# Attention scores, row steps and exponentials in another block order, with a look-ahead of one key tile and half of the scores split

## The chip, the core and the metric

The kernel runs on one core of one Trainium2 chip. The metric is the device time of one execution, in microseconds (us). The kernel before was timed in 3 runs: median 1334.1 us, lowest 1333.32, highest 1335.31.

## What is computed

One input `x` of 2048 rows and 512 columns goes through two branches, and a gate per row mixes them:

```python
# attention: 32 query heads of 16 columns share one key and one value head
q = (x @ wq).reshape(B, S, H, Dh); k = x @ wk; v = x @ wv
p = softmax(einsum("bhqd,bkd->bhqk", q, k) * Dh ** -0.5)
a = einsum("bhqk,bkd->bhqd", p, v).reshape(B, S, H * Dh) @ wo
# feed-forward, F = 1792
b = (silu(x @ w_gate) * (x @ w_up)) @ w_down
g = sigmoid((x * gate_w).sum(-1))
return g * a + (1 - g) * b
```

All in float32. The softmax is taken without subtracting a maximum; a flag computed beside it decides whether a slow path has to run, and it does not run here.

## The kernel before

**Tiles.** The kernel works head by head (32 heads) on key tiles of 128 keys, 16 to a head, numbered `u` from 0 to 511. For each `u` the scores of 128 keys against 2048 queries are needed. They are made in two score tiles (`j` = 0 and 1) of 1024 queries, each by two matmuls of 64 rows that run side by side (L727, output `pss`, one PSUM tile of two banks; there are two such tiles in rotation). ScalarE takes the exponential of a score tile into `pt` (L735). When a `u` is complete, the *mix* multiplies `pt` with the values and a column of ones and adds up into `po` (L747): four matmuls that run side by side in four column groups, each in two passes.

**Kinds.** A score tile is of kind A or H. Kind A: one exponential of 1024 columns from PSUM. Kind H (split): VectorE copies the second 512 columns out of PSUM into `pt` (L731), ScalarE takes the exponential of the first 512 from PSUM, and later of the other 512 in place in `pt`. The PSUM tile is free for the score tile after next once its exponential from PSUM and, for kind H, the copy are done.

**Feed-forward.** The feed-forward work and the query projections are cut into *jobs* of 12 or 15 matmuls (gate, up, down; L196, output `pf`, three PSUM tiles in rotation). During attention each matmul is cut into two halves of 64 rows: one *step* F runs a low half of one job beside a high half of another. The class `Halves` holds this pipeline: a low half starts when one of three tickets in `free` is due (7 clocks after a high half closed), and its high half starts `LAG` = 8 clocks after the low half's end; a 1x1 VectorE memset (`sign`, L470) orders the two. When a high half closes, VectorE takes `pf` out of PSUM (L299, L327, L390, L392); a list `HOLD` puts this behind the copy of a split score tile that comes within two steps.

**Order of the work.** It is written out by hand. `STEPS` is a string of 8 S (one score tile) and 16 F (one step) for a block of four key tiles; `KINDS` gives the kinds of its 8 score tiles, numbered 0 to 7; `EXPS` the order of the exponentials on ScalarE ("1d" from PSUM, "1s" in place, "|" the end of the block's steps). After the steps come ScalarE's tanh of the feed-forward, as much postponed VectorE work as fits a budget (`LATER`: normalization of a finished head; `DEFER`: silu, casts), then the mix of four key tiles. A block that mixes `u` to `u+3` scores `u+2` to `u+5`: the look-ahead is two key tiles. The first 32 key tiles run in a simpler loop of two key tiles; the block at the turn (`TURN`) scores five key tiles to build up the look-ahead; 118 blocks follow that are alike, and a last one that scores two.

**Stores in SBUF.** Six `pt` buffers (3 in `bp`, 3 in `bp2`), and three row chunks of the feed-forward sum `acc`; the fourth use of `acc` takes the place of chunk 0, which is stored to DRAM and read back at the end.

**The end.** Jobs that are left run with 128 rows. The last head is normalized, goes to DRAM and comes back transposed into chunks (L499), which ScalarE or GpSimd splits into a high and a low part (L501, L503, L504), and the output projection runs chunk by chunk (L118, L519).

Of the kernel before, what the change touches and what calls it, by code (L numbers as in the profile page):

```python
# [8 lines left out]
F32 = mybir.dt.float32  # L9
# [39 lines left out]
WRB = 2  # L49
BLOCK = 4  # L50
BEGIN = 16
STOP = 2
EARLY = 6
OUTS = (1, 2, 3, 0)
STEPS = "SSFFFFFSFSFFFSFFSFFFFFSS"
KINDS = "AHHAHAAA"
EXPS = ("0d", "1d", "2d", "3d", "4d", "5d", "1s", "4s", "2s", "|", "6d", "7d")
TURN = "SSFFFFSFS" + "FFS" * 5 + "FS"
BUDGET = 3.8
AHEAD = 6  # L60
# [3 lines left out]
def tile_gated_mix(ctx, tc, x, wq, wk, wv, wo, w_gate, w_up, w_down, gate_w, out):  # L64
# [213 lines left out]
    def open_acc():  # L278
        qpool.release()
        for name in ("accp", "bp2"):  # L280
            PAIR.append(tc.alloc_tile_pool(name=name, bufs=3, side="right"))

    def gate_up(n, c):
# [9 lines left out]

        def gate(ps):
            g = wp.tile([P, CH], F32, name="hs", bufs=2)
            if n == SPLIT:
# [102 lines left out]


    def jobs():
        late = []
        for m, c in enumerate(ORDER):
            for fs in GROUPS:
                ns = [m * NF + f for f in fs]
                new = [job for n in ns for job in gate_up(n, c)]
                if late and ns[-1] < NCH * NF - 1:
                    late[-1].after.append(lambda ns=ns: LOADS.extend([lambda n=n: load_w("d", n) for n in ns]))
                if fs[-1] == NF - 1:
                    if m < 2:  # L410
                        new[-1].after.append(lambda m=m: load_x_again(ORDER[m + 2]))
                for j, job in enumerate(new):
# [26 lines left out]
    class Halves:  # L439
# [6 lines left out]
        def step(self, more):  # L446
            for i in range(1, min(AHEAD, len(JOBS))):
                if not JOBS[0].ready() and JOBS[i].ready():
                    JOBS.insert(0, JOBS.pop(i))
            if (not self.low and JOBS and JOBS[0].ready() and (JOBS[0].only is None) == more and  # L450
                    self.free and min(self.free) <= self.clock):
                self.free.remove(min(self.free))
                self.low = [JOBS.pop(0), 0]
            if self.early and self.steps >= 4:
# [51 lines left out]
    def finish(c, pool):  # L506
        for i in range(TC):
# [3 lines left out]
            for j in range(parts):  # L511
# [7 lines left out]
                nc.vector.scalar_tensor_tensor(ot[:, w], ps[:, :D // parts], g_sb[:, t:t + 1], ACC[c][:, i, w],  # L519
                                               op0=ALU.mult, op1=ALU.add)  # L520
# [188 lines left out]
    with tc.tile_pool(name="bpool", bufs=2) as bp:  # L709
# [59 lines left out]
        NU = H * NT  # L769
        NB = NU // BLOCK  # L770
        COPY = []

        def feed(k, more=True):
            for _ in range(k):
                if JOBS and more or halves.busy():
                    halves.step(more)

        def block(k, first, last, steps, kinds, order):
            more = k < NB - STOP
# [4 lines left out]
            def emit():  # L784
                while order and order[0] != "|" and int(order[0][0]) < len(made):
                    i, how = int(order[0][0]), order.pop(0)[1]
                    pt, ps, other = made[i]
# [21 lines left out]
            assert not order and len(made) == len(tiles)  # L809
            left = BUDGET  # L810
            rest = NT // BLOCK - k % (NT // BLOCK)
            for _ in range(-(-len(LATER) // rest) if DEFER else 2):
                if LATER:
# [13 lines left out]
            FRESH.clear()  # L827
            for u in range(BLOCK * k, BLOCK * (k + 1)):
                mix(u)
            halves.clock += 2 * LONG  # L830

# [6 lines left out]
        with tc.manual_schedule():  # L838
# [24 lines left out]
            assert PAIR  # L863
            for k in range(2 * BEGIN // BLOCK, NB):
                u = BLOCK * k
                if k == 2 * BEGIN // BLOCK:
                    n = u + 6 - (u + 1)
                    block(k, u + 1, u + 6, TURN, "A" * 2 * n, [f"{i}d" for i in range(2 * n)])
                elif k == NB - 1:
                    block(k, u + 2, u + 4, STEPS, "AAAA", ("0d", "1d", "2d", "3d", "|"))  # L870
                else:
                    block(k, u + 2, u + 6, STEPS, KINDS, EXPS)
                h = u // NT
                if k % (NT // BLOCK) == 0 and 0 < h < H - 1:
                    load_head(h + 1)
# [9 lines left out]
    with tc.tile_pool(name="tpool", bufs=2) as tp, tc.tile_pool(name="rpool", bufs=1, side="right") as rp, \  # L885
# [112 lines left out]
```

## Time and profile before

| | us |
|---|---|
| median of 3 runs | 1334.1 |
| span of the profiled execution | 1332.6 |
| outside the span (median less span) | 1.5 |
| VectorE copies of split score tiles | 354, 692 ns each |
| exponentials from PSUM, 1024 columns / 512 columns | 670 / 354 |
| exponentials in place, 512 columns | 354 |
| longest wait of ScalarE, in total | 140.5, for scores |

The start (transposes, key and value projection, first query projections) takes some 49 us, the loop over the first 32 key tiles ends at 129, the blocks at 1260.6, and the end takes the remaining 72 us. In the chain of waits "PE po L747 x32" is the mix of one block, so the distance from one such row to the next is the time of a block. In a timeline a row holds the start, the duration, the engine, the line, the operation and in brackets how long the engine was idle before it and what ended that.

### The profile page before, as it was taken

How to read it: one execution, taken by the hardware profiler on the slowest of the kernel's cores; microseconds unless marked ns; L12 is line 12 of the kernel's file. 1: busy time of each engine (PE TensorE's matmuls, PEld its weight loads, DVE VectorE, ACT ScalarE, POOL GpSimd, SP SyncE). 2: the span in 40 equal slices, each digit the busy share in tenths (PEclk: the TensorE clock that was granted, in tenths of full speed). 3: DMA queues.
4: the chain of work that ended last, by engine and by line, in shares of the span. 5: the costliest groups of instructions: out<-in, count | busy, mean ns of one | idle time of the engine just before them, and what ended most of it. 6: DMA issues, size and time to landing. Idle time of an engine off the chain costs nothing.

```text
span 1332.6 us, 26698 instructions
## 1 busy us (share of the span) xinstructions
PE 1322.7 (99%) x10767; PEld 761.9 (57%) x10767; DVE 712.2 (53%) x1220; ACT 1069.0 (80%) x1475; POOL 225.4 (17%) x229
## 2 busy tenths in 40 slices
PE   9999999999999999999999999999999999999998
PEld 7655555555555555555555555555555555555587
DVE  4655565565546565555555555455455455546542
ACT  4578888888888888888888888888888888888601
POOL 5350221142032151142010000000000000001043
PEclk9999999999999999999999999999999999999999
DMA  8677021131125372264044342143132342143164
GB/s 286 206 227 241 27 61 36 45 92 53 45 93 176 113 241 68 92 211 138 33 134 161 103 159 84 53 145 102 37 114 64 104 161 82 52 147 108 39 207 151
DMA packets 101937, 156.29 MB, mean 117 GB/s; under 512 B 11824, under 2 KB 43312, under 8 KB 100144
## 3 DMA queue, kind: packets, MB, share of 16 engines
q1 hardware_dynamic: 100080, 154.31, 35.9%
q8 instruction: 88, 1.44, 0.5%
q10 hardware_dynamic: 1728, 0.20, 0.1%
q14 instruction: 41, 0.34, 0.1%
HBM read 98.37 MB, written 55.57 MB: 116 GB/s over the span
## 4 chain that ended last, share of the span: by engine, by line
PE 97%; ACT 1%; DVE 1%; issue 0%; DVEq 0%; ACTq 0%
PE pf L196 38%; PE po L747 34%; PE pss L727 20%; PE pf L118 4%; ACT pt L735 1%; PE pss L613 0%; PE po L600 0%; DVE xl L618 0%; PE pss L653 0%; DVE acc L390 0%; DVE ht L327 0%; DVE hs L299 0%; DVE wkv_l L109 0%; DVE pt L731 0%; ACT xh L617 0%
## 5 line engine op out<-in xcount | busy, mean ns | idle before, releaser
L735 ACT ACTIVATE pt<-pss 128x1024 f32<-128x1024 f32 (+1 forms) x1024 | 842.0, 876 | 173.7 <-PE pss L727 140.5
L731 DVE COPY pt<-pss 128x512 f32<-128x512 f32 x354 | 244.8, 692 | 419.8 <-PE pss L727 386.8
L747 PE MATMUL po<-pt,vaug 128*32 128x512 f32 x4096 | 467.6, 595 | 0.0
L727 PE MATMUL pss<-qs,ks 64*128 64x512 f32 x2048 | 395.1, 415 | 0.8 <-ACT pt L735 0.5
L727 PEld LDWEIGHTS pss<-qs,ks 64*128 64x128 f32 x2048 | 188.3, 184 | 220.1 <-ACT pt L735 183.8
L747 PEld LDWEIGHTS po<-pt,vaug 128*32 128x32 f32 x4096 | 119.2, 109 | 260.1 <-issue 254.9
L735 ACT ACTIVATE pt<-pt 128x512 f32<-128x512 f32 x354 | 195.6, 620 | 0.0
L196 PE MATMUL pf<-xh,wgl 64*128 64x512 f32 (+1 forms) x444 | 163.4, 392 | 0.0
L196 PE MATMUL pf<-xh,wgh 64*128 64x512 f32 (+1 forms) x444 | 161.8, 392 | 0.3
L196 PE MATMUL pf<-xl,wgh 64*128 64x512 f32 (+1 forms) x444 | 161.4, 390 | 0.0
L196 PE MATMUL pf<-xh,wuh 64*128 64x512 f32 (+1 forms) x440 | 158.4, 392 | 0.5 <-DVE sign L470 0.3
L196 PE MATMUL pf<-xl,wuh 64*128 64x512 f32 (+1 forms) x440 | 157.7, 390 | 0.0
L196 PE MATMUL pf<-xh,wul 64*128 64x512 f32 (+1 forms) x440 | 157.0, 391 | 0.0
L196 PE MATMUL pf<-wdh,hl 64*128 64x512 f32 (+1 forms) x411 | 137.0, 390 | 0.0
L196 PE MATMUL pf<-wdh,hh 64*128 64x512 f32 (+1 forms) x411 | 136.7, 391 | 0.0
L196 PE MATMUL pf<-wdl,hh 64*128 64x512 f32 (+1 forms) x411 | 136.6, 390 | 0.0
L756 DVE RECIPROCAL rsb<-rsb 128x128 f32<-128x128 f32 x128 | 116.9, 934 | 10.9 <-issue 8.8
L501 POOL CAST xh<-wraw 128x512 fp32r<-128x512 f32 x4 | 2.9, 726 | 505.2 <-DMA wraw<-o_d 505.2
L196 PEld LDWEIGHTS pf<-xh,wgh 64*128 64x128 f32 (+1 forms) x444 | 79.0, 185 | 8.8 <-issue 1.0
L196 PEld LDWEIGHTS pf<-xl,wgh 64*128 64x128 f32 (+1 forms) x444 | 79.1, 185 | 6.3
L196 PEld LDWEIGHTS pf<-xh,wuh 64*128 64x128 f32 (+1 forms) x440 | 77.1, 185 | 9.7 <-issue 2.1
L196 PEld LDWEIGHTS pf<-xh,wgl 64*128 64x128 f32 (+1 forms) x444 | 79.1, 185 | 5.7
(168 smaller groups left out, 1388.3 us busy)
## 6 DMA issues: line engine op xcount, KB each, us to landing
qs<-q_d SPq DMA_DIRECT2D x31, 512.0 KB, 5.1
q_d<-hh SPq DMA_DIRECT2D x28, 256.0 KB, 3.8
wraw<-in_B_w_gate_dram SPq DMA_DIRECT2D x28, 256.0 KB, 3.4
wraw<-in_B_w_up_dram SPq DMA_DIRECT2D x28, 256.0 KB, 3.1
wraw<-in_B_w_down_dram SPq DMA_DIRECT2D x28, 256.0 KB, 3.7
wgh<-w_d SPq DMA_DIRECT2D x28, 256.0 KB, 2.8
wgl<-w_d SPq DMA_DIRECT2D x28, 256.0 KB, 3.0
wuh<-w_d SPq DMA_DIRECT2D x28, 256.0 KB, 2.7
```

Of the source, the lines that this page charges most:

```text
L118: nc.tensor.matmul(ps, a, b, start=(i == 0), stop=(i == n - 1))
L196: ins = nc.tensor.matmul(self.ps, a, b, start=(i == 0 and opens), stop=(last and closes))
L501: nc.gpsimd.tensor_copy(OT[c][0][:, k, :], raw)
L727: nc.tensor.matmul(ps[:, b * CH:(b + 1) * CH], ks[rows, kt * P:(kt + 1) * P], QS[h][rows, j, :], start=True, stop=True)
L731: other = nc.vector.tensor_copy(pt[:, CH:], ps[:, CH:]) if half else None
L735: ins = nc.scalar.activation(pt[:, w], ps[:, w], AF.Exp, scale=SCALE)
L747: nc.tensor.matmul(po[c * 2 * DH:(c + 1) * 2 * DH, :], vaug[:, kt, :], pt[:, c * CH:(c + 1) * CH], start=(kt == 0), stop=(kt == NT - 1))
L756: nc.vector.reciprocal(rsb[:, w], rsb[:, w])
```

## The change

- The look-ahead goes from two key tiles to one: a block that mixes `u` to `u+3` scores `u+1` to `u+4`. The block at the turn scores four key tiles instead of five and has 12 F instead of 16; the last block scores three instead of two and goes on with full F steps (`STOP` 2 to 1; `feed` no longer stops when `more` is false).
- Split tiles are 1, 2, 5 and 6 instead of 1, 2 and 4. The sixth S stands one F later. The exponentials come in the order 0d 1d 2d 3d 4d 5d 5s 1s 2s, then, after the tanh, 6d 7d 6s. (The "T" in the table runs the tanh list, which is empty by then.)
- `pt` has seven buffers instead of six (`bp2` 4), `acc` two chunks instead of three. Chunk 1 is read back from DRAM into four buffers of the up weights at the end (`acc_again`), and the output chunks come in the order 2, 3, 1, 0 instead of 1, 2, 3, 0.
- The two loads of a row chunk (`load_x_again`) are no longer issued at once but put at the end of the list `LOADS`, behind down weights that wait there.
- A gate's end first runs postponed work of two feed-forward tiles earlier; a low half is picked from the first job that is ready; the VectorE budget goes from 3.8 to 3.87.

```diff
-OUTS = (1, 2, 3, 0)
-STEPS = "SSFFFFFSFSFFFSFFSFFFFFSS"
-KINDS = "AHHAHAAA"
+OUTS = (2, 3, 1, 0)
+STEPS = ("SSFFFFFSFSFFFSFFFSFFFFSS",)
+KINDS = ("AHHAAHHA",)
...
     def load_x_again(c):
         if c in ORDER:
-            for j, part in enumerate(new_x(c)):
-                nc.sync.dma_start(part.bitcast(F32), x_d[c - 2, j])
+            LOADS.extend([lambda j=j, part=part: nc.sync.dma_start(part.bitcast(F32), x_d[c - 2, j])
+                          for j, part in enumerate(new_x(c))])
...
-        for name in ("accp", "bp2"):
-            PAIR.append(tc.alloc_tile_pool(name=name, bufs=3, side="right"))
+        for name, bufs in (("accp", ACCS), ("bp2", PTL)):
+            PAIR.append(tc.alloc_tile_pool(name=name, bufs=bufs, side="right"))
...
         def gate(ps):
+            while any(item[0] <= n - 2 for item in DEFER):
+                run(ACTS, len(ACTS))
+                i = min(i for i, item in enumerate(DEFER) if item[0] <= n - 2)
+                DEFER.pop(i)[2]()
...
+    def acc_again():
+        c = ORDER[NCH - ACCS - 1]
+        ACC[c] = [wp.tile([P, KD, P], F32R, name="wu" + x, bufs=2).bitcast(F32).rearrange("p k f -> p (k f)")
+                  for x in "hhll"]
+        for i in range(TC):
+            nc.sync.dma_start(ACC[c][i], a_d[c, :, i, :])
...
-            for i in range(1, min(AHEAD, len(JOBS))):
-                if not JOBS[0].ready() and JOBS[i].ready():
-                    JOBS.insert(0, JOBS.pop(i))
...
+            if not self.low and self.free and min(self.free) <= self.clock:
+                for i in range(min(AHEAD, len(JOBS)) if more else len(JOBS)):
+                    if JOBS[i].ready() and (JOBS[i].only is None) == more:
+                        self.free.remove(min(self.free))
+                        self.low = [JOBS.pop(i), 0]
+                        break
...
-            late = u > PTB * (BEGIN * 2 // PTB) and (u - 2 * BEGIN) % (2 * PTB) >= PTB
-            PT[u] = (PAIR[1] if late else bp).tile([P, S], F32, name="pt", bufs=PTB)
+            late = u > 2 * BEGIN and (u - 2 * BEGIN) % (PTB + PTL) >= PTB
+            PT[u] = (PAIR[1] if late else bp).tile([P, S], F32, name="pt", bufs=PTL if late else PTB)
...
-                    block(k, u + 2, u + 6, STEPS, KINDS, EXPS)
+                    block(k, u, n, u + 1, end, STEPS[k % len(SIZES)], KINDS[k % len(SIZES)], EXPS[k % len(SIZES)].split())
```

ScalarE's instructions in one of the like blocks before, from tile 6 of the block ahead on (`pt<-pss` is an exponential from PSUM, `pt<-pt` one in place; in brackets the engines whose semaphores an instruction waits for):

```order
L735 ACTIVATE pt<-pss 128x1024 [waits PE_49,Activation_49]
L735 ACTIVATE pt<-pss 128x1024 [waits PE_49] x2
L735 ACTIVATE pt<-pss 128x512 [waits PE_49] x2
L735 ACTIVATE pt<-pss 128x1024 [waits PE_49]
L735 ACTIVATE pt<-pss 128x512 [waits PE_49]
L735 ACTIVATE pt<-pss 128x1024 [waits PE_49]
L735 ACTIVATE pt<-pt 128x512 [waits DVE_49] x2
L735 ACTIVATE pt<-pt 128x512
```

The rows are tile 6, tiles 7 and 0, tiles 1 and 2, 3, 4, 5, and the second halves of 1, 4 and 2. The same engine in one of the like blocks of the changed kernel, from tile 0 on:

```order
L749 ACTIVATE pt<-pss 128x1024 [waits PE_49,Activation_49]
L749 ACTIVATE pt<-pss 128x512 [waits PE_49] x2
L749 ACTIVATE pt<-pss 128x1024 [waits PE_49]
L749 ACTIVATE pt<-pss 128x1024 [waits PE_49,Activation_49]
L749 ACTIVATE pt<-pss 128x512 [waits PE_49]
L749 ACTIVATE pt<-pt 128x512 [waits DVE_49]
L749 ACTIVATE pt<-pt 128x512 x2
L749 ACTIVATE pt<-pss 128x512 [waits PE_49]
L749 ACTIVATE pt<-pss 128x1024 [waits PE_49]
L749 ACTIVATE pt<-pt 128x512 [waits DVE_49]
```

Before, the exponential with two waits is that of tile 6, in all 118 like blocks, and tile 0 has two in 2 of them; now tile 0 has two in 117 of 118, and tile 4 in all. VectorE in one block before, from the copy of tile 1 on (`pt<-pss` are the copies of split tiles; the rest is feed-forward):

```order
L731 COPY pt<-pss 128x512 [waits PE_49]
L731 COPY pt<-pss 128x512 [waits PE_49,Activation_49]
L327 TENSOR_TENSOR ht<-ht,pf 128x512 [waits PE_49]
L731 COPY pt<-pss 128x512 [waits PE_49,Activation_49]
L470 MEMSET sign 1x1 [waits PE_49]
```

And one block of the changed kernel, from the copy of tile 1 on:

```order
L745 COPY pt<-pss 128x512 [waits PE_49,Activation_49]
L745 COPY pt<-pss 128x512 [waits PE_49]
L398 SCALAR_TENSOR_TENSOR acc<-pf,c_sb,acc 128x512 [waits PE_49]
L484 MEMSET sign 1x1 [waits PE_49]
L745 COPY pt<-pss 128x512 [waits PE_49,Activation_49] x2
```

Before, the copy of tile 2 has two waits in 67 of the 118 like blocks, and so has that of tile 4; now the copy of tile 2 has one wait in all of them, and the copies of tiles 5 and 6 have two in 65. On TensorE the feed-forward matmuls behind the last mix are 95 instead of 99: 11 steps that were still in the pipeline and seven jobs, instead of eight jobs.

More of the change, by code (lines that the diff above doesn't have):

```diff
@@ L774, in feed, with block @@
             for _ in range(k):
-                if JOBS and more or halves.busy():
+                if JOBS or halves.busy():
                     halves.step(more)
-        def block(k, first, last, steps, kinds, order):
+        def block(k, u0, size, first, last, steps, kinds, order):
             more = k < NB - STOP
@@ L809, in block @@
             assert not order and len(made) == len(tiles)
-            left = BUDGET
-            rest = NT // BLOCK - k % (NT // BLOCK)
-            for _ in range(-(-len(LATER) // rest) if DEFER else 2):
+            left = BUDGET * size / 4
+            rest = len([v for v, _ in SPANS if v >= u0 and v // NT == u0 // NT])
+            for _ in range(max(-(-len(LATER) // rest), 0 if DEFER else 2)):
                 if LATER:
@@ L863, in tile_gated_mix @@
             assert PAIR
[L864 to L870, printed above, removed]
+            for k, (u, n) in enumerate(SPANS):
+                end = min(u + n + 1, NU)
+                m = 2 * (end - u - 1)
+                if k == NB - 1:
+                    block(k, u, n, u + 1, end, STEPS[k % len(SIZES)], KINDS[k % len(SIZES)][:m],
+                          [e for e in EXPS[k % len(SIZES)].split() if e in "T|" or int(e[:-1]) < m])
+                elif k == 0:
+                    block(k, u, n, u + 1, end, TURN[n], "A" * m, [f"{i}d" for i in range(m)])
                 else:
-                    block(k, u + 2, u + 6, STEPS, KINDS, EXPS)
+                    block(k, u, n, u + 1, end, STEPS[k % len(SIZES)], KINDS[k % len(SIZES)], EXPS[k % len(SIZES)].split())
                 h = u // NT
-                if k % (NT // BLOCK) == 0 and 0 < h < H - 1:
+                if u % NT == 0 and 0 < h < H - 1:
                     load_head(h + 1)
```

38 lines of the change are left out of this document (23 added, 15 removed).

## The prediction

> **What bounds the kernel now.** First the busy shares of the engines, from the profile's page:
>
> ```profile
> PE 1322.7 (99%) x10767; PEld 761.9 (57%) x10767; DVE 712.2 (53%) x1220; ACT 1069.0 (80%) x1475; POOL 225.4 (17%) x229
> ```
>
> TensorE (PE) is never idle for long. How much of its time is avoidable shows in the chain of waits, whose "L747 x32" rows are the mixes; their distances are the blocks:
>
> ```profile
> 147.36 3.57 PE po L747 x32
> ...
> 161.01 1.14 PE pf L196 x10
> ...
> 259.96 3.57 PE po L747 x32
> 269.75 3.57 PE po L747 x32
> 279.29 3.57 PE po L747 x32
> ...
> 364.39 3.57 PE po L747 x32
> 373.74 3.57 PE po L747 x32
> 383.17 3.57 PE po L747 x32
> ...
> 1193.29 3.57 PE po L747 x32
> 1202.90 3.58 PE po L747 x32
> ...
> 1231.15 3.57 PE po L747 x32
> ```
>
> From 147.36 to 1231.15 are 115 blocks, 9.424 each. The block at 364.39 takes 9.35: 3.57 of mix, 24 steps of .23 (1.14 for five F, each two matmuls) and .26 of transitions. The change keeps 8 S, 16 F and the mix, so I take 9.35 as the floor of both kernels. Above it lie 115 × .074 = 8.5 us; that is all there is to win in the like blocks. It has three parts: blocks a little long (9.43 at 373.74), blocks with a stall (9.79 at 259.96, 9.61 at 1193.29), and a middle kind (9.54 at 269.75).
>
> **The small surplus: a copy with two waits.** The copy of tile 2 has one wait in the block at 364.39 and two in that at 373.74. The timelines of both, from S2 on:
>
> ```profile
> 369.60 0.41 PE L727 MATMUL pss<-qs,ks 64*128 64x512 f32 x2
> ...
> 370.08 0.69 DVE L731 COPY pt<-pss 128x512 f32<-128x512 f32 x1 [0.69 <-PE pss L727]
> ...
> 371.03 0.40 PE L727 MATMUL pss<-qs,ks 64*128 64x512 f32 x2
> ...
> 371.49 0.69 DVE L731 COPY pt<-pss 128x512 f32<-128x512 f32 x1 [0.72 <-PE pss L727]
> ```
>
> ```profile
> 378.97 0.40 PE L727 MATMUL pss<-qs,ks 64*128 64x512 f32 x2
> ...
> 379.50 0.69 DVE L731 COPY pt<-pss 128x512 f32<-128x512 f32 x1 [0.77 <-PE pss L727]
> ...
> 380.40 0.44 PE L727 MATMUL pss<-qs,ks 64*128 64x512 f32 x2
> ```
>
> The copy starts .53 after S2 instead of .48, so the PSUM tile comes free later; S4, six steps behind S2, takes .44 instead of .40. The block is .08 longer.
>
> **The stalls.** The timeline of the block at 259.96:
>
> ```profile
> 267.06 0.69 DVE L731 COPY pt<-pss 128x512 f32<-128x512 f32 x1 [0.72 <-PE pss L727]
> ...
> 267.67 0.74 DVE L390 TENSOR_SCALAR acc<-pf,c_sb 128x512 f32<-128x512 f32 x1
> ...
> 268.55 0.47 PE L196 MATMUL pf<-xh,wuh 64*128 64x512 f32 x1 [0.15 <-DVE sign L470]
> ```
>
> A high half has closed, but its evacuation (L390) stands behind the copy of tile 4. It ends at 268.41, only then can `sign` run, and the new low half starts at 268.55. Nine blocks have this, at .26 (1193.29) to .44 (259.96); I take .37, 3.3 in all. The middle kind, a half that closes early in the block, costs .19 (269.75) or less in ten blocks, some 1.5. Out of 8.5 there remain 3.7 for the 67 blocks with two waits on tile 2, .055 each.
>
> **The change, part by part.**
>
> *Copy of tile 2, one wait everywhere:* −67 × .05 = −3.3 (bounds 0 and .08 × 67 = −5.4; .05 is nearer to the remainder above).
>
> *Tile 4 becomes kind A:* its copy goes, and an evacuation there runs at once: −3.3 (bounds −2.3 and −4.0).
>
> *Tile 5 becomes kind H:* S7 needs the PSUM tile of S5, six steps behind, just as S4 stands to S2. The copy of tile 5 has two waits in 65 blocks. By the copy of tile 2 that is .05 × 65 = +3.2 (bounds 0, as S6 stands between, and .10, 6.5). An evacuation behind it has the drain to the mix as cover: +.5, five blocks at .1 (bounds 0 and 9 × .26 = 2.3).
>
> *Tile 0's exponential gets a second wait,* for ScalarE's own earlier work, in 117 blocks. Only the first two like blocks show this now. Timeline of the first, and of one with a single wait:
>
> ```profile
> 150.86 0.73 PE L727 MATMUL pss<-qs,ks 64*128 64x512 f32 x4
> ...
> 151.46 3.14 ACT L735 ACTIVATE pt<-pss 128x1024 f32<-128x1024 f32 x4 [0.76 <-PE pss L727]
> ...
> 152.88 0.39 PE L196 MATMUL pf<-xh,wul 64*128 64x512 f32 x1
> ```
>
> ```profile
> 169.63 0.73 PE L727 MATMUL pss<-qs,ks 64*128 64x512 f32 x4
> ...
> 170.17 2.21 ACT L735 ACTIVATE pt<-pss 128x1024 f32<-128x1024 f32 x3 [0.69 <-PE pss L727]
> ...
> 171.59 0.40 PE L196 MATMUL pf<-xl,wgh 64*128 64x512 f32 x2
> ```
>
> With two waits it starts .60 after S0 instead of .54, and the F behind S2 starts 2.02 after S0 instead of 1.96: S2 needs tile 0's PSUM tile, and TensorE is pinned to the end of that exponential. Behind it on ScalarE stand tiles 1 and 2, which S3 and S4 wait for, so nothing gives the .06 back. +.06 × 117 = +7.0 (bounds 0, if PE catches up, and .08 × 117 = 9.4). This is the largest term and rests on two blocks. Tile 4's second wait stands over four steps ahead of S6 with one exponential between: nothing.
>
> The Trainium skill (Perfetto Trace Analysis, "Identifying Dependency Chains") says that an instruction that waits for several engines may get EventSemaphore instructions ahead of it, which carry the further waits. The trace agrees with that, at .05 to .06 here.
>
> *One more split per block* on ScalarE and VectorE. The groups by shape:
>
> ```profile
> L735 ACT ACTIVATE pt<-pss 128x1024 f32<-128x1024 f32 x670 | 666.5, 1024 | 161.9 <-PE pss L727 140.2 <-DMA q_d<-hh 7.6 <-issue 1.1
> L731 DVE COPY pt<-pss 128x512 f32<-128x512 f32 x354 | 244.8, 692 | 419.8 <-PE pss L727 386.8 <-ACT pt L735 28.2
> L735 ACT ACTIVATE pt<-pss 128x512 f32<-128x512 f32 x354 | 211.0, 596 | 11.9 <-PE pss L727 0.3
> L735 ACT ACTIVATE pt<-pt 128x512 f32<-128x512 f32 x354 | 195.6, 620 | 0.0
> ```
>
> ScalarE's busy time rises by 211.0/354 + 195.6/354 − 666.5/670 = .15 a split, some 18 us over 118 blocks, against 140 of idle time before these scores; VectorE's by 118 × .692 = 82 us, to 60%. Both are hidden: 0. Without that cover ScalarE's part would be +18.
>
> *The block at the turn.* In the chain it is bound by ScalarE:
>
> ```profile
> 131.71 5.62 ACT pt L735 x6
> 137.88 3.57 PE po L747 x32
> ```
>
> It scores eight tiles instead of ten: two exponentials of .94 (5.62/6) go, 1.87, but six steps (two S, four F) run elsewhere, 6 × .23 = 1.38: −.5 (bounds −1.9 and 0).
>
> *Loads, buffers, the middle kind:* rows of `x` are wanted a whole chunk later, so their place behind down weights costs nothing; the buffers of `pt` and `acc` cause no wait that I see. The middle kind: +.2 (one block more or less at .19).
>
> *The end.* The chain, and the last splits on GpSimd, from the timeline:
>
> ```profile
> 1283.69 21.76 PE pf L118 x96
> ```
>
> ```profile
> 1282.80 1.29 POOL L504 TENSOR_TENSOR xl<-wraw,xh 128x512 fp32r<-128x512 f32 x1
> ...
> 1291.41 5.04 POOL L504 TENSOR_TENSOR xl<-td,xh 128x512 fp32r<-128x512 f32 x4 [7.31 <-ACT xh L503]
> ```
>
> The projection's matmuls take .227 (21.76/96). With four fewer behind the last mix there is .9 less cover. The first chunk's last piece is split at 1284.09 and wanted with the 12th matmul, 1286.2; the second's at 1296.45, wanted with the 60th, 1297.1. The spare of .65 goes and .25 is missing: +.3 (bounds 0 and 1.5, since the reload of chunk 1 joins the transfers here).
>
> **Sum.** −3.3 −3.3 +3.2 +.5 +7.0 −.5 +.2 +.3 = +4.1. The profiled execution has a span of 1332.6 and the median is 1334.1, 1.5 around the span, which I leave. On the median: 1338.2. A measurement of this kernel can tell .2%, 2.7 us, from no change.
>
> **The rivals.**
>
> *Not slower (R1).* PE catches up the .06 behind tile 0. For it: only two blocks show the delay, and such a block also had two waits on tile 2 to mix it with. Against: F after S2 moved by just .06. The sum loses 7.0: −2.9, 1331.2, faster.
>
> *Tile 5's copy hidden (R3),* as the S6 between gives it time: the sum loses 3.2: 1335.0, the same.
>
> *The mix waits for the in-place exponentials (R2).* They now come 5s, 1s, 2s, at the very end of the steps. From the timeline of a mix and the exponentials behind it:
>
> ```profile
> 703.45 3.64 PE L747 MATMUL po<-pt,vaug 128*32 128x512 f32 x32
> ...
> 712.21 1.66 ACT L735 ACTIVATE pt<-pt 128x512 f32<-128x512 f32 x3
> ```
>
> Tile 5's copy ends 1.15 after S5 (.46 + .69 by tile 4's above), then 5s and 1s take .55 each (1.66/3): 2.26 after S5. The mix starts seven steps and .12 of transition after S5, at 1.73, and needs 1s with its second key tile, .89 later: 2.62, spare .36. It decides if the weight load ahead of that group, one group (.45) earlier, waits as well: then .1 × 118 = 12, 1346 to 1350, slower still.
>
> *ScalarE becomes the bound (R4):* then the split's price shows, up to the 18 above in place of the 4.1: some 1350. Against: 140 us of idle time. The Trainium skill (Perfetto Trace Analysis, "Optimizing Scalar/DVE Operations") says that larger operations help where the engine is saturated, and that breaking them up may help where it is not but causes bubbles elsewhere. By the first half the change would lose; at 80% busy the trace speaks for the second half.
>
> **How the numbers follow.** Forecast .50 (its own range 1336 to 1341.5), R1 .21, R3 .13, R2 .10, R4 .06. R1 lies about at the bound of "faster" (1331.4), two thirds of it below: .15. The same: R3, the rest of R1 and the lowest part of the forecast, .28. Slower: .57. The range leaves out R2, R4 and the lower end of R1: 1330.5 to 1342.5.
>
> **What would show it.** Right: ordinary blocks at 9.41 instead of 9.35, F after S2 at 2.02 after S0 in nearly all; the 9.6 to 9.8 blocks gone; S7 at .44 in half the blocks. Wrong: ordinary blocks at 9.35 (R1), a gap inside the mix (R2), PE waiting for ScalarE in S3 to S7 (R4), a block floor below 9.35, which nothing here foresees, or a stall at the end above 1.5.

## The result, and the profile after

The changed kernel takes 1346.19 us (median of 4 runs, 1344.49 to 1347.19), the kernel before in the same comparison 1334.7. The ratio is 1.0085, with a 95% interval of 1.0074 to 1.0097: 11.5 us slower. The forecast was 1338.2 with a range of 1330.5 to 1342.5. The direction was right, the size was not. The profiled span is 1344.5, 11.9 longer than before.

The busy shares tell little, as before: TensorE 99%, VectorE up from 53 to 59% by the extra copies, ScalarE from 80 to 81%.

```profile
PE 1331.0 (99%) x10782; PEld 779.0 (58%) x10782; DVE 786.8 (59%) x1342; ACT 1088.3 (81%) x1596; POOL 225.1 (17%) x229
```

The chain of waits of the changed kernel shows the blocks (the mix is now on line 761):

```profile
419.48 3.58 PE po L761 x32
428.91 3.57 PE po L761 x32
438.41 3.57 PE po L761 x32
...
580.80 3.57 PE po L761 x32
...
600.90 3.57 PE po L761 x32
...
1254.70 3.57 PE po L761 x32
1263.63 3.91 PE po L761 x32
```

An ordinary block takes 9.43 (at 419.48) or 9.50 (at 428.91), where it was 9.35 or 9.43. One block is 10.60 long: from 580.80 to 600.90 are two blocks, and the first has 9.50. The last mix takes 3.91.

The rows make four stretches, and these say where 11.9 us went. Before stands ahead of the arrow:

| stretch | before → after | difference |
|---|---|---|
| start to the first mix of a block, the turn with it | 137.8 → 135.4 | −2.4 |
| the 118 like blocks | 1112.1 → 1119.2 | +7.1 |
| the block that mixes ahead of the last mix | 7.0 → 8.9 | +1.9 |
| last mix to the end | 75.6 → 81.0 | +5.3 |

The turn and the last block were forecast at −.5 together, and −2.4 and +1.9 come to −.5. That agreement is luck. Of the −2.4, .5 lie ahead of the first mix of the simpler loop (54.25 before, 53.72 after), in the start, which varies from run to run. From that mix on, the turn gives −1.84, as forecast (−1.87), and the last block costs 1.94 instead of 1.38: +.1 together. The blocks were forecast at +4.3 and the end at +.3.

**The blocks.** S0 to S7 are the steps that make the scores of tiles 0 to 7. The timeline of the block at 428.91 shows S0, tile 0's exponential with its two waits, and the F behind S2:

```profile
432.41 0.73 PE L741 MATMUL pss<-qs,ks 64*128 64x512 f32 x4
...
433.01 3.13 ACT L749 ACTIVATE pt<-pss 128x1024 f32<-128x1024 f32 x4 [1.12 <-PE pss L741]
...
434.43 0.39 PE L198 MATMUL pf<-wdh,hh 64*128 64x512 f32 x1
```

The exponential starts .60 after S0 and the F 2.02 after it, as in the two early blocks of before. The trace shows where the .06 goes: ahead of each of the 269 exponentials from PSUM with two waits stands an EVENT_SEMAPHORE instruction on ScalarE, which starts .06 (median) earlier, and ahead of each of the 160 copies with two waits stands one on VectorE, .065 earlier. Of the exponentials and copies with one wait only three have such an instruction ahead of them. The second difference lies at the end of the block. First the block at 419.48 (9.43), then that at 428.91 (9.50), from S5 to the mix:

```profile
427.12 0.41 PE L741 MATMUL pss<-qs,ks 64*128 64x512 f32 x2
...
427.58 0.69 DVE L745 COPY pt<-pss 128x512 f32<-128x512 f32 x1 [0.19 <-PE pss L741]
...
428.27 0.64 PE L741 MATMUL pss<-qs,ks 64*128 64x512 f32 x4
...
428.84 0.64 PE L761 MATMUL po<-pt,vaug 128*32 128x512 f32 x4
```

```profile
436.54 0.41 PE L741 MATMUL pss<-qs,ks 64*128 64x512 f32 x2
...
437.07 0.69 DVE L745 COPY pt<-pss 128x512 f32<-128x512 f32 x1 [0.63 <-PE pss L741]
...
437.69 0.72 PE L741 MATMUL pss<-qs,ks 64*128 64x512 f32 x4
...
438.34 0.64 PE L761 MATMUL po<-pt,vaug 128*32 128x512 f32 x4
```

Tile 5's copy starts .46 or .53 after S5. S6 and S7 then take .64 or .72, and the mix starts .57 or .65 behind S6: the .07 of the copy's second wait goes through whole.

**The end.** VectorE's timeline behind the last mix, before the change (the mix ends at 1260.51) and after it (it ends at 1267.54):

```profile
1260.65 0.69 DVE L765 COPY osb<-po 128x512 f32<-128x512 f32 x1 [2.25 <-PE po L747]
...
1262.14 3.39 DVE L756 RECIPROCAL rsb<-rsb 128x128 f32<-128x128 f32 x4
...
1273.97 0.98 DVE L109 TENSOR_TENSOR hl<-ht,hh 128x512 fp32r<-128x512 f32 x1
```

```profile
1270.31 0.75 DVE L398 SCALAR_TENSOR_TENSOR acc<-pf,c_sb,acc 128x512 f32<-128x512 f32 x1 [1.39 <-PE pf L198]
1270.98 0.68 DVE L779 COPY osb<-po 128x512 f32<-128x512 f32 x1
...
1272.95 3.39 DVE L770 RECIPROCAL rsb<-rsb 128x128 f32<-128x128 f32 x4
...
1284.32 1.02 DVE L111 TENSOR_TENSOR hl<-ht,hh 128x512 fp32r<-128x512 f32 x1
```

And TensorE's row at that time:

```profile
1284.34 0.73 PE L198 MATMUL pf<-td,hh 128*128 128x512 f32 x2 [3.59 <-DVE hh L110]
```

Before, the copy of the last head out of `po` starts .14 behind the mix. After, it is issued behind the steps that are still in the pipeline, and stands 3.4 behind the mix, after an evacuation that waits for those steps. The normalization (four reciprocals, 3.39) comes 3.4 later with it, and behind it the casts that make the last `hh` and `hl`. The last down matmuls want these: TensorE stands still for 3.59 us. The last mix itself takes .34 more, since its weight loads wait twice for ScalarE's in-place exponentials (.21 at 1264.77 and .32 at 1265.29).

### The profile page after: what moved, and what is told of

Read it like the earlier page. It is cut to its first block, busy times and chain, and to the rows that moved or that the text cites. A ratio compares the mean times of both kernels' runs of the same rounds, so it can differ in the third digit from the quotient of the medians.

```text
span 1344.5 us, 27205 instructions
## 1 busy us (share of the span) xinstructions
PE 1331.0 (99%) x10782; PEld 779.0 (58%) x10782; DVE 786.8 (59%) x1342; ACT 1088.3 (81%) x1596; POOL 225.1 (17%) x229
## 4 chain that ended last, share of the span: by engine, by line
PE 97%; DVE 2%; ACT 1%; issue 0%; DVEq 0%; ACTq 0%
PE pf L198 37%; PE po L761 34%; PE pss L741 21%; PE pf L120 4%; PE pss L627 0%; ACT pt L749 0%; DVE rsb L770 0%; PE po L614 0%; DVE hl L111 0%; DVE hh L110 0%; DVE xl L632 0%; PE pss L667 0%; DVE rsb L780 0%; DVE ht L337 0%; DVE pt L745 0%
## 5 line engine op out<-in xcount | busy, mean ns | idle before, releaser
L749 ACT ACTIVATE pt<-pss 128x1024 f32<-128x1024 f32 (+1 forms) x1024 | 783.0, 823 | 144.5 <-PE pss L741 125.3
L745 DVE COPY pt<-pss 128x512 f32<-128x512 f32 x475 | 328.1, 691 | 396.1 <-PE pss L741 391.6
L741 PE MATMUL pss<-qs,ks 64*128 64x512 f32 x2048 | 404.0, 423 | 1.4 <-DVE sign L484 1.0
L741 PEld LDWEIGHTS pss<-qs,ks 64*128 64x128 f32 x2048 | 192.4, 184 | 217.4 <-ACT pt L749 189.1
L749 ACT ACTIVATE pt<-pt 128x512 f32<-128x512 f32 x475 | 272.7, 621 | 17.5 <-DVE pt L745 10.7
L761 PEld LDWEIGHTS po<-pt,vaug 128*32 128x32 f32 x4096 | 131.3, 109 | 246.4 <-issue 222.3
L198 PE MATMUL pf<-xh,wul 64*128 64x512 f32 (+1 forms) x440 | 160.7, 390 | 0.0
L198 PE MATMUL pf<-wdh,hh 64*128 64x512 f32 x416 | 136.2, 390 | 0.0
L198 PE MATMUL pf<-wdl,hh 64*128 64x512 f32 x416 | 135.0, 390 | 0.0
L198 PE MATMUL pf<-wdh,hl 64*128 64x512 f32 x416 | 134.6, 390 | 0.0
L198 PEld LDWEIGHTS pf<-xh,wgh 64*128 64x128 f32 (+1 forms) x444 | 80.3, 185 | 8.0 <-issue 0.5
```

The lines of the kernel that those rows point to most:

```text
L198: ins = nc.tensor.matmul(self.ps, a, b, start=(i == 0 and opens), stop=(last and closes))
L741: nc.tensor.matmul(ps[:, b * CH:(b + 1) * CH], ks[rows, kt * P:(kt + 1) * P], QS[h][rows, j, :], start=True, stop=True)
L745: other = nc.vector.tensor_copy(pt[:, CH:], ps[:, CH:]) if half else None
L749: ins = nc.scalar.activation(pt[:, w], ps[:, w], AF.Exp, scale=SCALE)
L761: nc.tensor.matmul(po[c * 2 * DH:(c + 1) * 2 * DH, :], vaug[:, kt, :], pt[:, c * CH:(c + 1) * CH], start=(kt == 0), stop=(kt == NT - 1))
```

## The experiments

The table gives for each kernel the median, the ratio to the kernel before (each was compared with runs of it on the same chip), the four stretches of the profiled run, and three mean distances in a like block between the starts of one step and the next (of the later matmul of each step, over the like blocks, about 100 of 118, in which all matmuls of the steps are on record).

| kernel | us | ratio (95%) | first mix | 118 blocks | last block | end | S2 to F | S4 to F | S7 to mix |
|---|---|---|---|---|---|---|---|---|---|
| before | 1334.7 | 1 | 137.8 | 1112.1 | 7.0 | 75.6 | .245 | .260 | .328 |
| changed | 1346.2 | 1.0085 (1.0074–1.0097) | 135.4 | 1119.2 | 8.9 | 81.0 | .306 | .234 | .373 |
| 1 order 5s 2s 1s | 1375.0 | 1.0300 (1.0286–1.0314) | 135.7 | 1146.9 | 9.2 | 81.3 | .243 | .233 | .376 |
| 2 six `pt` | 1342.6 | 1.0060 (1.0046–1.0073) | 138.3 | 1115.7 | 8.9 | 80.3 | .241 | .266 | .366 |
| 3 end first | 1342.4 | 1.0055 (1.0041–1.0069) | 135.8 | 1119.8 | 9.0 | 77.0 | .307 | .234 | .373 |
| 4 before, 1s 2s 4s | 1342.4 | 1.0055 (1.0041–1.0069) | 137.2 | 1119.8 | 7.1 | 75.2 | .308 | .260 | .329 |
| 5 order 2s 1s 5s | 1340.8 | 1.0050 (1.0037–1.0064) | 135.0 | 1113.4 | 8.9 | 81.4 | .244 | .248 | .373 |
| 6 split 1 2 4 5 | 1353.1 | 1.0137 (1.0121–1.0152) | 136.0 | 1126.7 | 9.0 | 81.0 | .240 | .247 | .364 |
| 7 split 1 2 | 1363.7 | 1.0221 (1.0207–1.0235) | 134.9 | 1137.2 | 8.9 | 79.3 | .243 | .233 | .433 |
| 8 split 1 2 4 5, end, gate | 1349.6 | 1.0110 (1.0095–1.0126) | 135.0 | 1127.2 | 9.0 | 76.8 | .241 | .247 | .363 |
| 9 as 5, one look more | 1335.7 | 1.0009 (1.0000–1.0018) | 136.0 | 1108.4 | 8.9 | 82.4 | .236 | .239 | .334 |
| 10 as 9, end first | 1332.4 | .9982 (.9972–.9991) | 138.2 | 1108.8 | 8.9 | 77.6 | .236 | .236 | .334 |
| 11 before, one look more | 1335.4 | 1.0006 (.9997–1.0015) | 137.8 | 1111.5 | 7.0 | 76.6 | .236 | .246 | .328 |
| 12 as 11, no hold at 4 | 1332.1 | .9981 (.9972–.9990) | 137.4 | 1109.2 | 7.0 | 76.5 | .236 | .247 | .329 |
| 13 old steps and kinds | 1346.9 | 1.0091 (1.0076–1.0106) | 135.3 | 1119.3 | 9.0 | 80.8 | .303 | .234 | .329 |
| 14 as 10, budget 3.4 | 1333.1 | .9990 (.9981–.9999) | 135.3 | 1109.4 | 8.9 | 77.6 | .236 | .238 | .335 |

The first mix starts at 134.9 to 136.0 in all kernels with the look-ahead of one but two (138.2 and 138.3), so the start by itself is uncertain by 3 us in a single profile; the other columns don't depend on it.

The theory behind them has three parts: the second wait of tile 0's exponential costs .06 in every block; the second wait of tile 5's copy costs .07 in some half of them; the end lost 5 us to VectorE's order. The main rival is that the waits are bystanders, and the new split and order cost the time by themselves.

### Tile 0's second wait: runs 1, 2, 4 and 5

Whether tile 0's exponential has the second wait depends on what was last written to its `pt` buffer, so an order of in-place exponentials or a number of buffers switches it on or off without touching the steps. Run 1:

```diff
-EXPS = ("0d 1d 2d 3d 4d 5d 5s 1s 2s | 6d T 7d 6s",)
+EXPS = ("0d 1d 2d 3d 4d 5d 5s 2s 1s | 6d T 7d 6s",)
```

> The changed kernel with the in-place exponentials in the order 5s 2s 1s instead of 5s 1s 2s, and nothing else. Only tile 0's exponential changes its waits: one in 117 of 118 like blocks instead of two; tile 4's and tile 5's copy keep theirs. Theory (the second wait of tile 0 goes through to the block): the F behind S2 comes 1.96 instead of 2.02 after S0, blocks are 9.36 and 9.43 instead of 9.43 and 9.50, -7.1 us against the changed kernel's 1346.2, so 1339. Rival A (the extra .06 comes from the new order or from ScalarE's extra split, the wait is a bystander): 1346, blocks as in the changed kernel. Rival B (the mix is the next to wait, as 1s now ends last, some 1.1 after the mix began while its key tile is due at .89): up to +.2 a block, 1346 to 1370.

The step from S2 to F falls to .243, as the theory has it, but the kernel is 29 us slower than the changed one: rival B, with 118 × .30 = 35 us. Its profile shows the place. ScalarE's three in-place exponentials end at 427.92, 1s as the last; the mix begins at 426.80; its weights for the next key tile wait for ScalarE until 427.97:

```profile
426.25 1.67 ACT L749 ACTIVATE pt<-pt 128x512 f32<-128x512 f32 x3
...
426.80 3.94 PE L761 MATMUL po<-pt,vaug 128*32 128x512 f32 x32
...
427.97 0.26 PEld L761 LDWEIGHTS po<-pt,vaug 128*32 128x32 f32 x5 [0.17 <-ACT pt L749]
```

The chain of this run has mixes of 3.87 to 3.91 where the changed kernel has 3.57. Run 2 has `PTL = 3` in place of 4.

> The changed kernel with six pt buffers instead of seven. Tile 0's exponential has one wait, the copy of tile 2 two in 66 of the like blocks (as before the change), all else the same. Theory: -7.1 for tile 0 and +3.1 for tile 2's copy (F behind S4 .026 later on average), 1342.2. Rival A (waits are bystanders): 1346. Rival C (the seventh buffer was needed, the exponentials wait for the mix): slower than 1346, with idle time of ScalarE before tile 6 put down to the mix.

It came at 1342.6, .4 from the theory's number; the 118 blocks lose 3.5 of the expected 4.0. S2 to F falls by .065, S4 to F rises by .032 (tile 2's copy has its two waits back). Run 4 does the opposite to the kernel before:

```diff
-EXPS = ("0d", "1d", "2d", "3d", "4d", "5d", "1s", "4s", "2s", "|", "6d", "7d")
+EXPS = ("0d", "1d", "2d", "3d", "4d", "5d", "1s", "2s", "4s", "|", "6d", "7d")
```

> The kernel before with its in-place exponentials in the order 1s 2s 4s instead of 1s 4s 2s, and nothing else. Tile 0's exponential then has two waits in 117 like blocks (two blocks before); all other counts stay. Theory: F behind S2 2.02 instead of 1.96 after S0, +7 us, 1341 to 1342. Rival A (the wait is a bystander): 1334.5, no change.

It is 7.6 us slower than before, 118 blocks take 7.7 more, and S2 to F goes from .245 to .308. From its timeline, in the order S0, tile 0, F behind S2 (.61 and 2.02 after S0):

```profile
425.49 0.73 PE L727 MATMUL pss<-qs,ks 64*128 64x512 f32 x4
...
426.10 1.51 ACT L735 ACTIVATE pt<-pss 128x1024 f32<-128x1024 f32 x2 [0.76 <-PE pss L727]
...
427.51 0.40 PE L196 MATMUL pf<-wdh,hh 64*128 64x512 f32 x1
```

Run 5 takes the wait away in the changed kernel and keeps 1s off the end of the order (`2s 1s 5s`).

> The changed kernel with the in-place exponentials in the order 2s 1s 5s instead of 5s 1s 2s. Tile 0's exponential has one wait as in the first run (order 5s 2s 1s), but 1s ends second and so in time for the mix; tile 5's copy keeps its two waits in 65 blocks. Theory: F behind S2 at .245 instead of .306, the mix 3.57 again, -7.1: 1339. If the mix stall of the first run came from something else than the end of 1s, the mix stays at 3.88 and the time near 1375. If waits are bystanders: 1346.

1340.8, with the mix at 3.57 again; .54 and 1.96 in its timeline:

```profile
421.57 0.73 PE L741 MATMUL pss<-qs,ks 64*128 64x512 f32 x4
...
422.11 2.21 ACT L749 ACTIVATE pt<-pss 128x1024 f32<-128x1024 f32 x3 [0.78 <-PE pss L741]
...
423.53 0.39 PE L198 MATMUL pf<-xh,wul 64*128 64x512 f32 x1
```

The 118 blocks lose 5.8 of the 7.1 expected. The rest fits S4 to F: the copy of tile 2 now has two waits in 26 blocks, and the step grew by .014 on average (1.7). The wait was switched on in one kernel and off in two orders and one buffer count, and the step from S2 to F followed each time by .06: this part is shown. The traces say the same of a copy's second wait, within one kernel: in the kernel before, S4 to F takes .280 in the 57 blocks with two waits on tile 2's copy and .234 in the 41 with one; in the changed kernel, S7 to the mix takes .40 in the 58 with two waits on tile 5's copy and .34 in the 42 with one.

### Tile 5's copy: runs 6, 7, 8 and 9

Run 6 splits tile 4 rather than tile 6, so that tile 5's copy is the second of VectorE into its buffer and has one wait:

```diff
-KINDS = ("AHHAAHHA",)
-EXPS = ("0d 1d 2d 3d 4d 5d 5s 1s 2s | 6d T 7d 6s",)
+KINDS = ("AHHAHHAA",)
+EXPS = ("0d 1d 2d 3d 4d 5d 2s 1s 4s 5s | 6d T 7d",)
```

> The changed kernel with tiles 1, 2, 4 and 5 split instead of 1, 2, 5 and 6, in-place exponentials 2s 1s 4s 5s and then 6d 7d. The number of splits stays at four; tile 0's exponential and tile 5's copy have one wait each (tile 4's copy two in 66, nine steps ahead of S6). Theory: -7.1 for tile 0 and -5.3 for tile 5's copy (the step from S7 to the mix falls from a mean of .373 to .33), up to +2 for evacuations behind tile 4's copy: 1334 to 1336. Rival (it is the split of tile 5 itself that S7 waits for, not the copy's second wait): the step from S7 to the mix stays at .37 and the time at 1339.

The expectation failed: 1353. More than half of its blocks are near the floor, 9.36 (two distances in its chain):

```profile
711.75 3.57 PE po L761 x32
721.11 3.57 PE po L761 x32
730.47 3.57 PE po L761 x32
```

Others have 9.6 and more, such as the one ahead of these. There VectorE copies a finished head out of `po` between tile 4's and tile 5's copy, and tile 5's starts at 710.41, .74 behind S5 (709.67) instead of .46; S7 waits for it:

```profile
709.21 0.69 DVE L745 COPY pt<-pss 128x512 f32<-128x512 f32 x1 [0.43 <-PE pss L741]
...
709.67 0.40 PE L741 MATMUL pss<-qs,ks 64*128 64x512 f32 x2
709.82 0.68 DVE L779 COPY osb<-po 128x512 f32<-128x512 f32 x1
...
710.41 0.68 DVE L745 COPY pt<-pss 128x512 f32<-128x512 f32 x1
```

The other blocks of this run show the same: in 44 of the 118 the copy of a finished head or an evacuation of `pf` stands between the copies of tiles 4 and 5, and these take 9.63 to 11.26 (mean 9.81); the other 74 take 9.39 in the mean. The 44 lose 19 us against the floor, about what the expectation left out. So the run tells the theory and its rival apart less well than it should have, but the mechanism is the same: S7 waits for the end of that copy. Run 7 has no copy of tile 5 (`AHHAAAAA`, in-place exponentials `2s 1s`).

> The changed kernel with only tiles 1 and 2 split, in-place exponentials 2s 1s. Tile 0's exponential has one wait; there is no copy of tile 5. Theory of the waits: S7 now waits for tile 5's whole exponential, which ScalarE ends some 5.6 us after S0, when S7 is due: between -12 (1334) and, at .1 to .2 a block for S7, 1346 to 1358. Rival (ScalarE's extra splits cost the time, .15 each): two splits fewer, -12 to -35 and no wait at S7, 1311 to 1334.

1363.7, above the theory's range: S7 now waits for tile 5's whole exponential in every block (the step to S7 .397 instead of .233, S7 to the mix .433; blocks of 9.63). The rival that ScalarE's extra splits cost the time is refuted. Two splits fewer free ScalarE (77% busy) and make the kernel 17 us slower. The Trainium skill (Perfetto Trace Analysis, "Optimizing Scalar/DVE Operations") says that breaking up an instruction may help where the engine isn't saturated but makes others wait; the 17 us agree. Run 8 put two more edits on run 6: the end of run 3, and a gate's end without the loop that runs postponed work.

> The kernel of the run with tiles 1, 2, 4 and 5 split, with two more edits: the last head is normalized ahead of the steps left in the pipeline (-3.8 where it was done alone), and a gate's end no longer runs postponed work of two feed-forward tiles earlier (one block of 10.60 instead of 9.50, -1.1). If the causes add up: 1334 to 1336 less 4.9, 1329 to 1331, faster than the kernel before by .3 to .4%. If the stalls only move: 1334 to 1340.

It came at 1349.6: it gained the end (81.0 to 76.8), but not its expected total, since it stands on run 6; its longest block, 11.26, stayed, so the loop in `gate` is not what makes such blocks. Run 9 took the wait from tile 5's copy in another way, on top of run 5:

```diff
+    seen = cpool.tile([1, 1], F32, name="seen")
...
                     made.append(score(*tiles[len(made)], kinds[len(made)] == "H"))
+                    if len(made) == 4 and "s" in "".join(order):
+                        nc.vector.tensor_copy(seen, PT[tiles[0][0]][0:1, 0:1])
```

> The run with the order 2s 1s 5s (1340.8), with one more VectorE instruction a block: after tile 3's scores it copies one element of tile 0's exponential into a scratch. VectorE has then waited for ScalarE once, off the path, and the copies of tiles 2, 5 and 6 have one wait in all blocks. The split of tile 5 stays. Theory (the second wait of tile 5's copy is what S7 and the mix wait for): the step from S7 to the mix falls from a mean of .373 to .33, -5, and F behind S4 from .248 to .234, -1.6: 1334 to 1336. Rival (the split itself, or the two waits of S7, cost it): 1340 to 1342, the step stays at .37; the extra instruction costs nothing.

1335.65, 5.1 less than run 5. S7 to the mix falls from .373 to .334, and almost all blocks stand at 9.37, with tile 5 still split:

```profile
398.84 3.57 PE po L762 x32
408.21 3.57 PE po L762 x32
```

So the second wait costs it, not the split, and 118 × .039 = 4.6 us is its price.

### The end: runs 3 and 10

```diff
+            run(COPY, 1)
+            while LATER:
+                LATER.pop(0)[1]()
             while halves.busy():
                 halves.step(False)
-            run(COPY, 1)
             settle()
```

> The changed kernel with the last head's copy out of po and its whole normalization issued on VectorE ahead of the steps that are left in the pipeline, instead of behind them. Theory (the end lost 5 us because VectorE's normalization came 3.4 us later behind the last mix and the feed-forward's casts stood behind it, so that TensorE stood still for 3.6 us and then ran at a granted clock of .50 for about 4): the gap before the last down matmuls goes and the time falls by 4 to 6 us, to 1340 to 1342. Rival (four matmuls fewer behind the last mix, or the reload of chunk 1, make the end longer): at most 1 us changes, 1345 to 1347, and the gap moves to another line.

1342.4, 3.8 less; the end falls from 81.0 to 77.0 and the other stretches move by .6 at most. Of the standstill .82 is left, and the `hl` that it waits for took 1.65 (the last section shows why):

```profile
1282.17 1.65 DVE L111 TENSOR_TENSOR hl<-ht,hh 128x512 fp32r<-128x512 f32 x1
```

```profile
1283.88 0.50 PE L198 MATMUL pf<-td,hl 128*128 128x512 f32 x1 [0.82 <-DVE hl L111]
```

Fewer matmuls and the reload of chunk 1 are as in the changed kernel, so they are not what these 3.9 were lost to. The end is still 1.4 longer than before: .3 of it is the last mix, and what part of the rest the fewer matmuls have was not tested. Run 10 puts the same edit on run 9.

> The same, and the last head is normalized ahead of the steps left in the pipeline (-3.8 where it was done alone). If all causes add up: 1330 to 1332, faster than the kernel before by .2 to .35%. If the rival of the run without the end is right: 1336 to 1338, slower.

1332.37, just above the expected range, ratio .9982 (.9972 to .9991): with these three waits gone the changed kernel is faster than the kernel before by .2%. That this is the look-ahead's gain is not shown (run 12).

### The kernel before, mended: runs 11 and 12

> The kernel before with one VectorE instruction more a block, which copies one element of tile 0's exponential behind tile 1's scores, so that the copies of tiles 2 and 4 have one wait in all blocks instead of two in 66. Theory: F behind S4 falls from .260 to .234, -3.1: 1331 to 1332. Rival (the second wait is a bystander): 1334.9.

The edit is that of run 9, behind tile 1 (`len(made) == 2`). Expected were −3.1; the 118 blocks lost .7 and the median nothing. S4 to F fell only from .260 to .246. The trace shows what holds it: the new instruction waits for the end of tile 0's exponential, which comes only shortly ahead of S2, and VectorE stands still for it (.11 in the median). In 29 of the 98 complete blocks an evacuation of `pf` comes behind it and ahead of tile 2's copy, which then starts .55 after S2, and the step takes .276; in the other 69 the copy starts .47 after S2 and the step takes .235, as with one wait. So the edit pays back, in this place, part of what it gains; run 9's stands behind tile 3, where the exponential has ended and VectorE never stands still for it. Run 12 adds this:

```diff
-if "S" in steps[i + 1:i + 3] and kinds[len(made):len(made) + 1] == "H":
+if "S" in steps[i + 1:i + 3] and kinds[len(made):len(made) + 1] == "H" and len(made) != 4:
```

> The same, and an evacuation of pf no longer stands behind the copy of tile 4. Theory (the stalls of the kernel before are evacuations behind that copy): the nine blocks of 9.6 to 9.8 go, the mean of the sixth F behind S5 falls from .250 to .230, another -2 to -3: 1328 to 1330. Rival (the copy of tile 4, later now, makes S6 wait, or the stall moves to another step): 1331 to 1335.

3.3 less than run 11, 1332.1 (.9981, .9972 to .9990); the time itself is above the expected 1328 to 1330, as run 11's was. The step on which a low half starts late falls from .250 to .232. Nine blocks of run 11 have an evacuation behind tile 4's copy and take 9.63 to 9.81; the same blocks now take 9.36 to 9.38. So nine stalls of before were evacuations behind tile 4's copy. This version, too, beats both kernels, and differs from run 10 by less than a measurement tells: once both kernels are mended, no gain of the look-ahead of one tile is left to see.

### The change without its new steps, and the long block: runs 13 and 14

Run 13 is the changed kernel with the old `STEPS`, `KINDS` and order of in-place exponentials; the seven `pt` buffers, the loads and the end stay as changed.

> The changed kernel with the STEPS, KINDS and in-place order of the kernel before (tiles 1, 2 and 4 split, 1s 4s 2s): look-ahead of one tile, buffers, loads and end as changed, no new split. Tile 0's exponential has two waits in 117 blocks (two blocks before the change), tile 2's copy one in all. Theory: tile 0 +7, the end +5, the turn and the last block together 0, the evacuations behind tile 4's copy as before the change, no wait at S7: the changed kernel less 5.3 plus 2 to 3, 1343 to 1344. Rival (the look-ahead itself is harmless and the new split and order cost the time): 1335 to 1340, F behind S2 at .245.

1346.9 (1343.1 to 1348.2), 3 above the theory's number and as slow as the whole change. Tile 0's second wait (.303) and the end (80.8) are there, S7 has none (.329), and instead a late low half costs more than before (the step .270 instead of .250): 14 blocks are above 9.6, one of them 11.3. So the new split and order give back about what S7 costs, and the loss comes with the rest of the change: the look-ahead with its buffers, and the end. Run 14 tests where the long blocks come from.

> The run with one look more for VectorE and the end first (1332.4), with a VectorE budget of 3.4 for postponed work at a block's end instead of 3.87. Theory (the blocks of 10.1 to 10.6 come from postponed VectorE work at a block's end that runs past S0 and holds the copy of tile 1): both long blocks go, -1.5, 1330.5 to 1331.5, the rest stays. Rival (a DMA or GpSimd makes them): they stay, 1332 to 1333. If the budget is too small for the work, it collects and other blocks grow: above 1333.

1333.1, so the expected gain did not come. The two long blocks of run 10 went, but one of 11.31 came elsewhere. The budget moves them, it doesn't cure them.

## Why the prediction was wrong, point by point

| step of the sum | forecast | measured |
|---|---|---|
| tile 0's second wait | +7.0 | +7.2 (118 × .061); the step moved by .062 to .065 in runs 1, 2, 4 and 5 |
| tile 2's copy, one wait | −3.3 | −3.1 (118 × .026) |
| tile 5's copy | +3.2 | +5.3 (118 × .045), of which 4.6 its second wait |
| tile 4's copy gone | −3.3 | −2.2 (118 × .019, on the step where a low half starts) |
| evacuation behind tile 5's copy | +.5 | not seen by itself |
| the middle kind | +.2 | not seen by itself |
| a block of 10.60 | not in the sum | +1.1 to 1.2 |
| turn and last block | −.5 | +.1 (−1.84 + 1.94); −.5 more is the start |
| the end | +.3 (0 to 1.5) | +5.3 |

**The step that failed is the end.** The prediction gave it +.3 and at most 1.5, from the matmuls that cover GpSimd's splits, and it measured +5.3. VectorE's order there was never read. Its `COPY` of the last head moved behind the steps that drain the pipeline, and the casts before the change had hardly any spare. From TensorE's timeline of the kernel before:

```profile
1275.01 0.50 PE L196 MATMUL pf<-td,hl 128*128 128x512 f32 x1
```

The `hl` of 1273.97 (shown above) ended at 1274.95, and this is the matmul that wants it, .06 later. 3.4 us later is then nearly 3.4 us of TensorE, and the slow clock behind it comes on top (below). The .34 of the last mix is also in the 5.3. Run 3 got 3.9 of it back; the remaining 1.0 is open (in run 3 a standstill of .82, for an `hl` that took 1.65, is part of it).

**Mis-sized: tile 5's copy.** The mechanism was right, with the same six steps as between S2 and S4. The price per block was nearer to that of the row (.07), about .06 between blocks with two waits and with one, and not the .05 that was taken as the remainder of other terms. S7 has only the mix behind it, and nothing gives the time back.

**Rivals.** R1 (the .06 is caught up) is refuted by runs 2, 4 and 5. R3 (tile 5's copy is hidden by S6) by run 9. R2 (the mix waits for in-place exponentials) does not happen in the like blocks of the order 5s 1s 2s, whose mixes take 3.57, but it does in the last block (3.91), and in run 1, where 1s ends one in-place exponential (.55) later, it costs 35 us. R4 (ScalarE's splits) by run 7.

By its profiled time the change was forecast at +4.1 and came at +11.9, 7.8 apart. The end (5.0), tile 5 (2.1), the long block (1.2), tile 4 (1.1) and tiles 0 and 2 (.2 each) less the evacuation (.5) make 9.3. The other −1.5 is the forecast middle kind (−.2) and small changes of many steps, which were not followed up; the start's −.5 and the +.6 of turn and last block cancel.

## What to carry to other kernels

Where TensorE is pinned to the engine ahead of it, count the waits of the instruction that releases it, not only what it computes: a second wait that is long satisfied still cost .06 us in 117 of 118 blocks. Another order of the same work removed it on ScalarE, and on VectorE one idle instruction that takes the wait earlier did; placed where the engine had to stand still for it (run 11), that instruction lost part of its gain again. When a loop is drained differently at its end, read the queue of every engine there, not only of the one whose work was counted. An order of exponentials by deadline of the mix is worth more than any of these: the wrong one of three cost 35 us.

## What the runs showed of the hardware that was not expected

**TensorE came back from a pause at half its clock.** The changed kernel's windows around the standstill, with the granted clock in the column behind POOL:

```profile
1280.80:1284.30 3.50, 0.00 (x0) 0.00 (x0) 2.65 (x4) 0.63 (x1) 3.05 (x4) 1.00 0.47 123
1284.30:1286.30 2.00, 1.64 (x4) 1.03 (x5) 1.19 (x2) 0.00 (x0) 1.92 (x2) 0.80 0.16 52
1286.30:1288.40 2.10, 2.10 (x6) 1.65 (x5) 0.58 (x1) 0.00 (x0) 0.71 (x2) 0.50 0.96 286
1288.40:1290.50 2.10, 2.10 (x9) 1.68 (x8) 0.25 (x1) 0.00 (x0) 1.36 (x2) 0.87 0.81 292
```

TensorE is idle for 3.5 us, and the granted clock then falls: .80 and .50 in the next two windows, and .87 in the one behind them. From 1284.3 to 1288.4 it starts 10 matmuls where 18 fit at full speed (4.1/.227). The 10 would have taken 2.3 us; the rest is 1.8 us, an idle stretch of .32 for `hl` among them. In run 3, with .82 idle, the clock stayed at 1.00. The Trainium skill (TensorE: Matmul & The Clock Gate, "Part 1: The HAM clock gate (the "warmup" mystery)") gives half the clock after an idle window of about 3.4 us, and full speed after about as long a busy one; both agree with these rows.

**A VectorE instruction waited for one of GpSimd.** In the block of 10.60 of the changed kernel:

```profile
592.11 1.29 POOL L111 TENSOR_TENSOR wul<-wraw,wuh 128x512 fp32r<-128x512 f32 x1
...
592.42 1.53 DVE L337 SCALAR_TENSOR_TENSOR ht<-hs,ht 128x512 f32<-128x512 f32 x1
...
594.50 1.36 POOL L111 TENSOR_TENSOR wdl<-wraw,wdh 128x512 fp32r<-128x512 f32 x1
...
594.74 1.67 DVE L111 TENSOR_TENSOR hl<-ht,hh 128x512 fp32r<-128x512 f32 x1
...
596.34 1.29 DVE L745 COPY pt<-pss 128x512 f32<-128x512 f32 x2
...
597.16 0.50 PE L741 MATMUL pss<-qs,ks 64*128 64x512 f32 x2 [0.95 <-DVE sign L484]
```

Elsewhere such instructions take .67 to .69 in the mean. Here they end .55 behind the end of GpSimd's (593.40 and 595.86), whatever their start. The copy of tile 1 then starts at 596.34, and S3 is .95 late: this is how a long block comes about. The traces of all 16 kernels agree: 158 of these instructions (`hl` from `ht` and `hh`, `ht` from `hs` and `ht`) took more than .95, each had started while a GpSimd instruction ran, and each ended .54 to .55 behind it. None of the 1579 that started with GpSimd idle took so long. Apart from runs 6 and 8, where two instructions between the copies of tiles 4 and 5 also make such blocks, every like block above 10.1 holds one or two of them. The Trainium skill (SBUF — State Buffer, "SBUF: two separate sides") has VectorE's instructions with two inputs in SBUF and GpSimd's take a shared pair of ports as an exclusive lock; the rows fit that. No run took GpSimd's work out of such a block, so that the long blocks would go without it is not tested.
